# One store of ScalarE in place of two, and w3 in three transfers, in a decode kernel on Trainium2

## Chip, cores, metric

One core of a Trainium2 chip (trn2). The metric is the device time of one execution in microseconds (us). The program runs on one core only; runs called "fast" below are those not more than 1.5% above the fastest of the same kernel, and ratios use only them.

## What is computed

A decode step for four sequences: layer norm of x, attention over a window of cached keys and values, and a gated feed-forward block, all added to x.

```
xn  = layernorm(x)                                   # x: 4 x 1 x 640
q   = xn @ wq                                        # 32 heads of 192
p   = softmax(q k^T / sqrt(192))                     # the last 2048 of 8192 keys, per sequence and head
a   = (p v) @ wo
f   = (silu(xn @ w1) * (xn @ w3)) @ w2               # 640 -> 1536 -> 640
out = x + a + f                                      # 4 x 1 x 640, bf16
```

The K and V windows are 2 x 32 loads of 3.1 MB; with the weights the kernel reads 223 MB.

## The kernel before

All loads but the small one of x, which ScalarE issues, are issued by SyncE (`nc.sync.dma_start`) from a hand-written schedule. w1, w3 and w2 take turns in one buffer (a pool with one slot). w1 and w3 are loaded in two pieces each: rows of 2 and of 3 times 1536 bf16 values per partition, that is 6144 and 9216 bytes.

```python
    def ffn_load(name, w):
        wt = fpool.tile([P, KC, F], BF16, tag="w", name=name)      # KC = 5, F = 1536
        for k0, k1 in ((0, KC // 2), (KC // 2, KC)):
            nc.sync.dma_start(out=wt[:, k0:k1, :].rearrange("p k n -> p (k n)"),
                              in_=w.rearrange("(p kc) n -> p kc n", kc=KC)[:, k0:k1, :].rearrange("p k n -> p (k n)"))
        ffn[name] = wt
    # ... (cut)
    add(15, 0, ffn_load, "w3", B_w3)      # issued in slot 15 of the schedule
    add(23, 7, ffn_in, "w3")              # used in slot 23
```

The result is accumulated in PSUM in two halves of 320 columns: the first in partitions 0 to 3, the second in partitions 32 to 35. At the end two engines cast the halves and two queues store them:

```python
    NR = CT + B                                                     # CT = 32, B = 4, N0 = 320
    res = [ppool.tile([NR, N0], BF16, tag="pr", name="res") for _ in range(2)]
    nc.scalar.copy(out=res[1][CT:NR, :], in_=acc[CT:NR, :])         # ScalarE (ACT)
    nc.vector.tensor_copy(out=res[0][0:B, :], in_=acc[0:B, :])      # VectorE (DVE)
    out_v = out.rearrange("b s d -> (b s) d")
    nc.scalar.dma_start(out=out_v[:, N0:D], in_=res[1][CT:NR, :])
    nc.sync.dma_start(out=out_v[:, 0:N0], in_=res[0][0:B, :])
```

One thing is not in the source. The library gives each transfer one of eight completion semaphores in turn ("lanes" below, numbers 100, 102, 103, 106, 107, 108, 109, 110 in the trace). A transfer waits until the one eight places earlier on the same lane has landed. At the end of the program SyncE waits for the lanes in a fixed order, two semaphores at a time, and (109, ..) and (110, ..) are the last two waits. Before the change there are 88 transfers; the two stores are the last and fall on lanes 109 and 110.

Of the kernel before, what the change touches and what calls it, by code (L numbers as in the profile page):

```python
# [11 lines left out]
BF16 = mybir.dt.bfloat16  # L12
# [38 lines left out]
def kernel(  # L51
# [19 lines left out]
    nc = tc.nc  # L71
    P = 128
    B, Sq, D = A_x.shape
    _, H, Sk, Dh = A_k_cache.shape
    W = min(4096, max(256, Sk // 4))
    F = B_w1.shape[1]
    KC = D // P
# [9 lines left out]
    CT = 32  # L87
# [3 lines left out]
    N0 = D // 2  # L91
# [16 lines left out]
    ppool = ctx.enter_context(tc.tile_pool(name="pr", bufs=PBUFS))  # L108
# [36 lines left out]
    for k0 in range(0, KC, 2):  # L145
        n = min(2, KC - k0)
        wt = vpool.tile([P, 2, H * Dh], BF16, tag="vt")
        nc.sync.dma_start(out=wt[:, 0:n, :].rearrange("p k n -> p (k n)"),
                          in_=wq_v[:, k0:k0 + n, :].rearrange("p k n -> p (k n)"))
# [77 lines left out]
    acc = ps_acc.tile([P, N0], FP32, name="acc")  # L227
# [120 lines left out]
    hT = const.tile([P, FC, CT], BF16, name="hT")  # L348
    ffn = {}

    def ffn_load(name, w):
        wt = fpool.tile([P, KC, F], BF16, tag="w", name=name)
        for k0, k1 in ((0, KC // 2), (KC // 2, KC)):
            nc.sync.dma_start(out=wt[:, k0:k1, :].rearrange("p k n -> p (k n)"),
                              in_=w.rearrange("(p kc) n -> p kc n", kc=KC)[:, k0:k1, :].rearrange("p k n -> p (k n)"))
        ffn[name] = wt
# [33 lines left out]
    def add(slot, phase, fn, *args):  # L390
        sched[slot].append((phase, len(sched[slot]), fn, args))
# [28 lines left out]
    for hg in range(NG - 2):  # L420
        a = ((hg + 1) * HG - 1) * GQ + L + 3
        add(hg * HG * GQ + 8, 0, wo_load, hg)
        add(a, 6, ge_proj, hg, 0, RPP // 2)
        add(a + 1, 6, ge_proj, hg, RPP // 2, RPP)
    add(3, 0, ffn_load, "w1", B_w1)
    add(11, 7, ffn_in, "w1")
    add(11, 9, ffn_silu)
    add(15, 0, ffn_load, "w3", B_w3)
    add(23, 7, ffn_in, "w3")
    add(23, 9, ffn_h)  # L430
    add(16, 6, x_add, 0)
# [19 lines left out]
        for phase, _, fn, args in sorted(sched[s], key=lambda e: (e[0], e[1])):  # L451
            fn(*args)

    NR = CT + B
    res = [ppool.tile([NR, N0], BF16, tag="pr", name="res") for _ in range(2)]
    nc.scalar.copy(out=res[1][CT:NR, :], in_=acc[CT:NR, :])
    nc.vector.tensor_copy(out=res[0][0:B, :], in_=acc[0:B, :])
    out_v = out.rearrange("b s d -> (b s) d")
    nc.scalar.dma_start(out=out_v[:, N0:D], in_=res[1][CT:NR, :])
    nc.sync.dma_start(out=out_v[:, 0:N0], in_=res[0][0:B, :])  # L460


# [28 lines left out]
```

## Time and profile before

| | before |
|---|---|
| time, median of 3 runs | 526.6 us (526.47 to 526.67) |
| span of the profiled run | 524.4 us |
| busy share of the DMA engines' time, load queue | 99.2% |
| PE (TensorE), DVE (VectorE), ACT (ScalarE) busy | 69%, 66%, 9% of the span |

The page of the kernel before shows what limits it: the DMA row and the GB/s row (the span in 40 equal slices, 9 means 90% or more busy), the load queue q1 with its share of the time of 16 engines, and the chain of waits that ended last.

```profile
DMA  9999999999999999999999999999999999999996
GB/s 385 426 441 429 426 431 436 427 435 429 433 427 437 431 428 437 427 431 436 429 430 439 423 439 429 433 429 435 429 429 435 432 429 435 429 435 431 424 428 258
DMA packets 12285, 223.26 MB, mean 426 GB/s; under 512 B 1373, under 2 KB 1513, under 8 KB 3177
...
q1 hardware_dynamic: 12248, 222.96, 99.2%
...
DMA 61%; DVE 21%; PE 15%; ACT 2%; issue 1%; SPq 0%
DMA kt<-in_A_k_cache_dram 52%; DVE pr L244 14%; PE ps L255 8%; DMA vt<-in_A_v_cache_dram 4%; DMA w<-in_B_w_dram 4%; DVE sc L263 3%; PE qps L210 3%; PE po L328 3%; DMA x_sb<-in_A_x_dram 1%; DVE z L299 1%; ACT ex L291 1%; PE mt L285 1%; ACT L
```

The DMA engines are busy in all slices but the last, and the chain is mostly DMA. The compute engines wait: the waits of the kernel before (engine, line, what it waited for: total us, times, longest) have DVE idle for 108.5 us before its products until K has landed.

```profile
DVE pr L244 <- DMA kt<-in_A_k_cache_dram: 108.5, 29, 8.3
```

So a change can gain here in three ways: less work for the DMA engines, fewer gaps in their supply, or a shorter tail after the last load. The tail of the kernel before, from the timeline (start, duration, engine, line, operation; `ACTq` and `SPq` are the issue of a transfer by that engine's queue):

```profile
520.99 0.71 PE L231 MATMUL acc<-w,hT 128*4 128x320 bf16 x8 [0.15 <-DMA w<-in_B_w_dram]
...
521.73 0.48 DVE L457 CAST res<-acc 4x320 bf16<-4x320 f32 x1 [2.07 <-PE acc L231]
521.76 0.42 ACT L456 CAST res<-acc 4x320 bf16<-4x320 f32 x1 [4.59 <-PE acc L231]
522.21 0.28 ACTq L459 DMA_DIRECT2D out_dram<-res  x1
522.24 0.35 SPq L460 DMA_DIRECT2D out_dram<-res  x1
```

Stretches of the last loads of the kernel before, one us each (after the time: busy us of PE, PEld, DVE, ACT, POOL; then granted clock, DMA share, GB/s):

```profile
518.00:519.00 1.00, 1.00 (x21) 0.66 (x17) 0.17 (x1) 0.00 (x0) 0.00 (x0) 1.00 0.65 268
519.00:520.00 1.00, 0.45 (x10) 0.18 (x6) 0.62 (x2) 0.00 (x0) 0.00 (x0) 1.00 0.50 205
520.00:521.00 1.00, 0.84 (x14) 0.44 (x12) 0.00 (x0) 0.00 (x0) 0.00 (x0) 1.00 0.40 154
521.00:522.00 1.00, 0.70 (x8) 0.33 (x7) 0.27 (x1) 0.24 (x1) 0.00 (x0) 1.00 0.00 1
```

The DMA engines do not end together: in the last three us of loads the share falls from 0.65 to 0.40, because some engines have finished their part of the last transfers before others: the 16 counts of the last w2 load came between 518.01 and 521.35 us. The remainder of the tail is not on the page. The records of DMA packets and semaphores in the same trace give it:

```
store by ACT (lane 109): 4 packets of 640 B start 522.975 ... 523.051; last count 523.414
store by SP  (lane 110): 4 packets of 640 B start 523.074 ... 523.148; last count 523.593
SyncE passes its wait for 109 at 523.43, for 110 at 523.61; barriers until 524.43
```

The issue of the w3 loads (two, at 65.84 us) on SyncE's queue is followed by a long pause of that queue:

```profile
65.20 0.55 SPq L132 DMA_DIRECT2D vt<-in_A_v_cache_dram  x1
65.84 1.02 SPq L354 DMA_DIRECT2D w<-in_B_w_dram  x2
83.02 0.54 SPq L125 DMA_DIRECT2D kt<-in_A_k_cache_dram  x1
```

(L125, L132 and L354 are the lines of `load_k`, `load_v` and `ffn_load`.)

### The profile page before, as it was taken

To read this page: it belongs to the slowest core of one execution; us is meant where nothing else is said; L and a number is where in the kernel's file an instruction comes from. 1 tells how busy PE (TensorE), PEld (TensorE's weight loads), DVE (VectorE), ACT (ScalarE), POOL (GpSimd) and SP (SyncE) were. 2 spreads that over 40 slices of the span, in tenths; PEclk is the share of its full clock that TensorE was granted. 3 is DMA by queue.
4 is the path that set the end of the run, shared out by engine and by line. 5 is a ranking of instruction groups with operands and counts; after the bars stand their busy time and mean duration, and the time that the engine had idled before them with its cause. 6 is when DMAs were issued, how large, how long until landed. Compare 5 with 4: busy or idle time off the path is not lost.

```text
span 524.4 us, 4738 instructions
## 1 busy us (share of the span) xinstructions
PE 359.4 (69%) x2306; PEld 73.8 (14%) x1613; DVE 346.0 (66%) x435; ACT 46.0 (9%) x144; POOL 1.1 (0%) x8
## 2 busy tenths in 40 slices
PE   0965966577746767667658767676686876685785
PEld 0000211111111111111111111111111111111122
DVE  3179755479657767677656876577666866677681
ACT  2111201000000000000000000000000000000001
POOL 0000000000000000000000000000000000000000
PEclk9979878969878999789887988699878898889888
DMA  9999999999999999999999999999999999999996
GB/s 385 426 441 429 426 431 436 427 435 429 433 427 437 431 428 437 427 431 436 429 430 439 423 439 429 433 429 435 429 429 435 432 429 435 429 435 431 424 428 258
DMA packets 12285, 223.26 MB, mean 426 GB/s; under 512 B 1373, under 2 KB 1513, under 8 KB 3177
## 3 DMA queue, kind: packets, MB, share of 16 engines
q1 hardware_dynamic: 12248, 222.96, 99.2%
q8 instruction: 15, 0.25, 0.2%
q14 instruction: 6, 0.04, 0.0%
q10 hardware_dynamic: 16, 0.01, 0.0%
HBM read 222.96 MB, written 0.01 MB: 425 GB/s over the span
## 4 chain that ended last, share of the span: by engine, by line
DMA 61%; DVE 21%; PE 15%; ACT 2%; issue 1%; SPq 0%
DMA kt<-in_A_k_cache_dram 52%; DVE pr L244 14%; PE ps L255 8%; DMA vt<-in_A_v_cache_dram 4%; DMA w<-in_B_w_dram 4%; DVE sc L263 3%; PE qps L210 3%; PE po L328 3%; DMA x_sb<-in_A_x_dram 1%; DVE z L299 1%; ACT ex L291 1%; PE mt L285 1%; ACT L291 0%; DVE oT L336 0%; DVE og L333 0%
## 5 line engine op out<-in xcount | busy, mean ns | idle before, releaser
L255 PE MATMUL ps<-pr,idb 128*128 128x512 bf16 x768 | 219.4, 429 | 146.2 <-DVE pr L244 146.1
L244 DVE TENSOR_TENSOR pr<-kt,qbc 128x3072 bf16<-128x3072 bf16 x128 | 223.4, 1746 | 108.5 <-DMA kt<-in_A_k_cache_dram 108.5
L263 DVE TENSOR_REDUCE sc<-ps 128x16 f32<-128x512 f32 x128 | 87.1, 680 | 2.3 <-PE ps L255 2.3
L307 PE MATMUL o_ps<-vt,z 128*8 128x384 bf16 x1024 | 54.4, 350 | 0.2 <-DVE z L299 0.2
L328 PE MATMUL po<-o_sb,sel_w 128*32 128x192 f32 x128 | 49.2, 518 | 0.6 <-ACT o_sb L310 0.6
L307 PEld LDWEIGHTS <-z 128*8 128x8 bf16 x1024 | 24.9, 90 | 91.4 <-issue 80.0
L310 ACT COPY o_sb<-o_ps 128x384 f32<-128x384 f32 x32 | 15.3, 479 | 187.2 <-PE o_ps L307 187.2
L299 DVE TENSOR_TENSOR z<-ex,mask_b 128x256 bf16<-128x256 bf16 x32 | 13.5, 423 | 25.6 <-ACT ex L291 25.6
L288 ACT COPY negm<-mt 128x1 f32<-128x1 f32 x32 | 5.1, 159 | 259.5 <-PE mt L285 259.5
L272 PEld LDWEIGHTS mt<-idf,lmax 128*1 128x1 f32 x32 | 3.5, 108 | 142.8 <-issue 141.8
L328 PEld LDWEIGHTS po<-o_sb,sel_w 128*32 128x32 f32 x128 | 14.0, 132 | 30.8 <-issue 29.3
L255 PEld LDWEIGHTS <-idb 128*128 128x128 bf16 x124 | 11.9, 96 | 38.1 <-issue 31.6
L210 PE MATMUL qps<-wt,xnT 128*128 128x512 bf16 x59 | 16.0, 433 | 0.6 <-DVE xnT L201 0.6
L285 PEld LDWEIGHTS mt<-ones_ff,gneg 1*128 1x128 f32 x64 | 9.4, 182 | 46.1 <-issue 21.6
L277 DVE TENSOR_REDUCE gmax<-mt 1x4 f32<-1x128 f32 x32 | 8.8, 276 | 7.2 <-PE mt L272 7.1
L216 DVE CAST qbc<-qps 128x512 bf16<-128x512 f32 x6 | 3.8, 684 | 13.4 <-PE qps L210 13.4
L285 PE MATMUL mt<-ones_ff,gneg 1*128 1x1 f32 x64 | 12.1, 256 | 0.6 <-DVE gneg L280 0.6
L315 PEld LDWEIGHTS po<-rsum,tot_w 128*32 128x32 f32 x64 | 4.4, 108 | 53.6 <-ACT ex L291 27.8
L272 PE MATMUL mt<-idf,lmax 128*1 128x128 f32 x32 | 11.5, 359 | 0.0
L291 ACT ACTIVATE ex<-sc,negm 128x64 bf16<-128x64 f32 x32 | 11.1, 348 | 1.0
L231 PE MATMUL acc<-wo_t,oT 128*4 128x320 bf16 x96 | 9.3, 298 | 0.5 <-DMA wo_t<-in_A_wo_dram 0.5
L199 PE MATMUL xnT_ps<-idb,xn 4*128 4x4 bf16 x5 | 0.4, 178 | 12.0 <-DVE xn L194 12.0
(53 smaller groups left out, 69.2 us busy)
## 6 DMA issues: line engine op xcount, KB each, us to landing
kt<-in_A_k_cache_dram SPq DMA_DIRECT2D x32, 3072.0 KB, 19.9
vt<-in_A_v_cache_dram SPq DMA_DIRECT2D x30, 3072.0 KB, 27.1
wo_t<-in_A_wo_dram SPq DMA_DIRECT2D x8, 960.0 KB, 21.0
wt<-in_A_wq_dram SPq DMA_DIRECT2D x2, 3072.0 KB, 13.1
vt<-in_A_v_cache_dram SPq DMA_DIRECT2D x4, 1536.0 KB, 23.2
w<-in_B_w_dram SPq DMA_DIRECT2D x2, 1152.0 KB, 32.5
wt<-in_A_wq_dram SPq DMA_DIRECT2D x1, 1536.0 KB, 19.6
w<-in_B_w_dram SPq DMA_DIRECT2D x2, 768.0 KB
```

What stands on the lines that cost most here:

```text
L210: nc.tensor.matmul(qp[:], lhsT=xnT[:, kc].rearrange("p a b -> p (a b)"), rhs=wq_rows[kc][:, (c0 + i) * QC:(c0 + i + 1) * QC], start=(kc == ...
L231: nc.tensor.matmul(acc[i * CT:i * CT + B, :], lhsT=lhsT, rhs=rhs[:, i * N0:(i + 1) * N0], start=first, stop=last)
L244: nc.vector.tensor_tensor(out=pr[:], in0=kts[h][:, g * JQ:(g + 1) * JQ, :], in1=qbc[:, h * Dh:(h + 1) * Dh].unsqueeze(1).to_broadcast([P, ...
L255: nc.tensor.matmul(ps[:], lhsT=idb[:], rhs=pr[:, :, kk * DD:(kk + 1) * DD], start=(kk == 0), stop=(kk == NK - 1))
L263: nc.vector.tensor_reduce(out=scs[h][:, g * JQ:(g + 1) * JQ], in_=pss.pop(u)[:], axis=AX.X, op=ALU.add)
L272: nc.tensor.transpose(out=mt[0:1, 0:P], in_=chs[h][0][:], identity=idf[:])
L285: nc.tensor.matmul(mt[:, P:P + 1], lhsT=gneg[:].rearrange("o p b -> o (p b)"), rhs=ones_ff[:], start=True, stop=True)
L291: nc.scalar.activation(out=ex[:], in_=scs.pop(h)[:], func=ACTF.Exp, bias=negm[:, 0:1], scale=SCALE, accum_out=rsum[:])
L299: nc.vector.tensor_tensor(out=z[:], in0=ex[:].unsqueeze(2).to_broadcast([P, NJ, B]), in1=mask_b[:].unsqueeze(1).to_broadcast([P, NJ, B]), ...
L307: nc.tensor.matmul(o_ps[c * CT:c * CT + 2 * B, :], lhsT=z[:, 2 * jj:2 * jj + 2, :], rhs=vt[:, 2 * jj:2 * jj + 2, :], start=(jj < 4), stop= ...
L310: nc.scalar.copy(out=o_sb[:], in_=o_ps[:])
L328: nc.tensor.matmul(po[sl, 0:Dh], lhsT=sel_w[:, par].rearrange("p a b -> p (a b)"), rhs=o_sb[:, par * Dh:(par + 1) * Dh].rearrange("p (r i) ...
```

## The change

Its intent: one transfer of whole rows in place of two half-row transfers from two queues, with one completion at the end instead of two; and one more load for w3, which among other things keeps the number of transfers at 88.

```diff
-    def ffn_load(name, w):
+    def ffn_load(name, w, *at):
         wt = fpool.tile([P, KC, F], BF16, tag="w", name=name)
-        for k0, k1 in ((0, KC // 2), (KC // 2, KC)):
+        for k0, k1 in zip((0,) + at, at + (KC,)):
 ...
-    add(3, 0, ffn_load, "w1", B_w1)
+    add(3, 0, ffn_load, "w1", B_w1, KC // 2)
-    add(15, 0, ffn_load, "w3", B_w3)
+    add(15, 0, ffn_load, "w3", B_w3, KC // 2, KC - 1)
 ...
-    NR = CT + B
-    res = [ppool.tile([NR, N0], BF16, tag="pr", name="res") for _ in range(2)]
-    nc.scalar.copy(out=res[1][CT:NR, :], in_=acc[CT:NR, :])
-    nc.vector.tensor_copy(out=res[0][0:B, :], in_=acc[0:B, :])
-    out_v = out.rearrange("b s d -> (b s) d")
-    nc.scalar.dma_start(out=out_v[:, N0:D], in_=res[1][CT:NR, :])
-    nc.sync.dma_start(out=out_v[:, 0:N0], in_=res[0][0:B, :])
+    res = ppool.tile([B, 2, N0], BF16, tag="pr", name="res")
+    nc.scalar.copy(out=res[:, 1, :], in_=acc[CT:CT + B, :])
+    nc.vector.tensor_copy(out=res[:, 0, :], in_=acc[0:B, :])
+    nc.scalar.dma_start(out=out.rearrange("b s d -> (b s) d"), in_=res[:].rearrange("b i n -> b (i n)"))
```

## The prediction

> **What bounds the kernel now.** The page's slice table has the DMA row at 9 (90% or more) in 39 of 40 slices, mean 426 GB/s; the queue table gives the load queue 99.2% of the 16 engines' time. The chain of waits is 61% DMA, mostly kt loads. PE (69%) and DVE (66%) have slack. The trace's packet records fit a line: 6144 B take 234 ns, 9216 B 347 ns, 12288 B 460 ns, so about 8 ns per packet plus bytes at 27 B/ns. Only three things can move the time: the DMA engines' work, a gap in their supply, or the tail after the last load.
>
> The tail, from the timeline: last w2 piece landed at 521.35 us, last matmul ends 521.70, the two casts (ACT 0.42, DVE 0.48 us) end 522.18 and 522.21, both stores are issued at 522.21 (ACT queue) and 522.24 (SP queue), their packets run 522.98 to 523.18, SyncE's end-of-program waits see the ACT store at 523.43 and the SP store at 523.61, and barriers run until 524.43.
>
> **w3 in three transfers.** Same bytes and order. The 128 packets of 9216 B become 128 of 6144 and 128 of 3072 B (estimate from the fit: 234 + 121 = 355 ns instead of 347). With 8 rows per engine that is 8 x 8 ns plus one more completion write of 9 ns, about 0.07 us of DMA time per engine. DMA is full, so this can reach the end: +0.07 us. The extra issue costs SyncE's queue about 0.5 us near 67 us, where it then idles until 83 us: free. w3 lands by 99 us and is first used at about 117 us, so PE gains nothing from finer pieces. Completion semaphores rotate over eight lanes; one more load shifts them, but near w3 the transfer eight back has long landed, and at the end the distance of eight is unchanged (one store fewer, one load more: still 88 transfers, and the store stays on the last lane waited for). The waits of the last wo and w2 loads (490.2, 497.5, 501.1, 504.8 us) stay.
>
> **One store.** The SP issue (0.35 us, parallel) goes. The casts write disjoint columns of four partitions. I expect no ordering between them: the q casts of ACT and DVE into one tile overlap in the timeline (21.28 to 21.87 and 21.50 to 22.19). The ScalarE store must now also wait for DVE's cast: issue at 522.25 to 522.30 instead of 522.21. The Trainium skill, "DMA: Bandwidth & Descriptors", section "Issuing engines are not separate DMA queues", says different issuers share the same 16 DMA engines, so two queues save only issue time; the trace agrees: SP's 640 B packets follow ACT's. Now four packets of 1280 B (55 ns, as the x load shows) replace eight of 640 B (29 ns). Completion should be seen at 523.47 to 523.55 instead of 523.61: -0.05 to -0.15 us.
>
> **Sum.** +0.07 - 0.10, about -0.03 us: inside the spread of the runs (0.2 us). Predicted 526.5 us, 8 in 10 between 526.2 and 526.9. Faster by over 2%: 0.003; within 2%: 0.994; slower by over 2%: 0.003.
>
> **Right if:** the same DMA share and GB/s; 3072 B packets at about 121 ns; last w2 landing within 0.3 us of 521.35; casts overlapping; store issued 0.03 to 0.1 us after DVE's cast; final completion 0.05 to 0.15 us earlier relative to the last matmul.
>
> **Wrong if:** the two casts are serialized by their common tile (+0.45 us); the shifted lanes make a load wait and the DMA row drops below 9 between 67 and 120 us; a single store takes over 1.4 us from issue to completion; or the uneven finish of the DMA engines (DMA share 0.65, 0.50, 0.40 in the last three us of loads) changes.

## The result, and the profile after

After: 526.51 us median of 6 runs (526.30 to 526.79). Before, with the three runs beside it: 526.48 us median of 6 (526.26 to 526.67). Ratio 1.000, 95% interval 0.9988 to 1.0013. A ratio here and below is the mean time of one kernel's fast runs over that of the other's of the same rounds, so it is not quite the ratio of the medians quoted.

The page after, the same rows:

```profile
DMA  9999999999999999999999999999999999999996
GB/s 388 422 441 427 431 429 434 427 435 429 435 427 432 434 428 437 427 433 431 433 428 441 423 437 429 433 431 433 426 434 431 434 433 431 431 431 432 425 427 260
DMA packets 12420, 223.26 MB, mean 426 GB/s; under 512 B 1384, under 2 KB 1520, under 8 KB 3440
...
q1 hardware_dynamic: 12384, 222.96, 99.2%
...
DMA 64%; DVE 21%; PE 12%; ACT 1%; issue 1%; SPq 0%
DMA kt<-in_A_k_cache_dram 52%; DVE pr L244 15%; PE ps L255 7%; DMA vt<-in_A_v_cache_dram 4%; DMA wt<-in_A_wq_dram 4%; DMA w<-in_B_w_dram 4%; DVE sc L263 3%; PE po L328 3%; PE qps L210 1%; DVE z L299 1%; ACT ex L291 1%; DVE oT L336 1%; PE mt
```

Busy share and GB/s are those of before; q1 has 136 packets more (128 of data, 16 completions for the extra load, less 8 of SyncE's store). The split of the chain between PE and DMA differs by three points, with equal spans; the chain alone is no measure of time here.

The tail after, from the timeline. `SPq` has gone from it:

```profile
520.99 0.71 PE L231 MATMUL acc<-w,hT 128*4 128x320 bf16 x8 [0.19 <-DMA w<-in_B_w_dram]
...
521.73 0.48 DVE L456 CAST res<-acc 4x320 bf16<-4x320 f32 x1 [4.51 <-PE acc L231]
521.77 0.42 ACT L455 CAST res<-acc 4x320 bf16<-4x320 f32 x1 [7.01 <-PE acc L231]
522.29 0.27 ACTq L457 DMA_DIRECT2D out_dram<-res  x1
```

The stretches of the last loads, as before:

```profile
518.00:519.00 1.00, 0.49 (x8) 0.18 (x4) 0.00 (x0) 0.00 (x0) 0.00 (x0) 1.00 0.65 270
519.00:520.00 1.00, 0.18 (x4) 0.13 (x5) 0.00 (x0) 0.00 (x0) 0.00 (x0) 1.00 0.48 196
520.00:521.00 1.00, 0.81 (x14) 0.41 (x11) 0.00 (x0) 0.00 (x0) 0.00 (x0) 1.00 0.41 159
521.00:522.00 1.00, 0.70 (x8) 0.33 (x7) 0.27 (x1) 0.23 (x1) 0.00 (x0) 1.00 0.00 0
```

And from the packet and semaphore records of this trace:

```
last w2 load counted complete: before 521.353, after 521.351
store by ACT (lane 110): 4 packets of 1280 B start 523.052, .094, .146, .197; last count 523.585
SyncE passes its wait for 110 at 523.60; barriers until 524.41
w3: 128 packets of 3072 B took 121 ns each, 256 of 6144 B 234 ns (w1 still has 128 of 9216 B, 347 ns)
```

From the end of the last matmul to SyncE's last wait for a store is 1.912 us before and 1.901 us after. The last load lands at the same time. In the tail nothing has moved by more than a tenth of a microsecond. Earlier, SyncE's queue issues three w3 loads in its pause, and single issues there shift by up to a microsecond (the v load from 65.20 to 66.26 us); this does not make the last load land later:

```profile
66.26 0.55 SPq L132 DMA_DIRECT2D vt<-in_A_v_cache_dram  x1
66.90 1.49 SPq L354 DMA_DIRECT2D w<-in_B_w_dram  x3
82.78 0.54 SPq L125 DMA_DIRECT2D kt<-in_A_k_cache_dram  x1
```

### The profile page after: what moved, and what is told of

Same layout as the page of the kernel before. It is cut to its first block, busy times and chain, and to the rows that moved or that the text cites. A ratio compares the mean times of both kernels' runs of the same rounds, so it can differ in the third digit from the quotient of the medians.

```text
span 524.4 us, 4737 instructions
## 1 busy us (share of the span) xinstructions
PE 357.6 (68%) x2306; PEld 73.9 (14%) x1613; DVE 345.4 (66%) x435; ACT 46.0 (9%) x144; POOL 1.1 (0%) x8
## 3 DMA queue, kind: packets, MB, share of 16 engines
q1 hardware_dynamic: 12384, 222.96, 99.2%
## 4 chain that ended last, share of the span: by engine, by line
DMA 64%; DVE 21%; PE 12%; ACT 1%; issue 1%; SPq 0%
DMA kt<-in_A_k_cache_dram 52%; DVE pr L244 15%; PE ps L255 7%; DMA vt<-in_A_v_cache_dram 4%; DMA wt<-in_A_wq_dram 4%; DMA w<-in_B_w_dram 4%; DVE sc L263 3%; PE po L328 3%; PE qps L210 1%; DVE z L299 1%; ACT ex L291 1%; DVE oT L336 1%; PE mt L285 0%; ACT L291 0%; DVE og L333 0%
## 5 line engine op out<-in xcount | busy, mean ns | idle before, releaser
L255 PE MATMUL ps<-pr,idb 128*128 128x512 bf16 x768 | 216.0, 423 | 144.7 <-DVE pr L244 144.7
L307 PE MATMUL o_ps<-vt,z 128*8 128x384 bf16 x1024 | 56.8, 362 | 0.2 <-DVE z L299 0.2
L210 PE MATMUL qps<-wt,xnT 128*128 128x512 bf16 x59 | 14.9, 410 | 1.3 <-DMA wt<-in_A_wq_dram 0.6
```

What stands on the lines that cost most here:

```text
L210: nc.tensor.matmul(qp[:], lhsT=xnT[:, kc].rearrange("p a b -> p (a b)"), rhs=wq_rows[kc][:, (c0 + i) * QC:(c0 + i + 1) * QC], start=(kc == ...
L255: nc.tensor.matmul(ps[:], lhsT=idb[:], rhs=pr[:, :, kk * DD:(kk + 1) * DD], start=(kk == 0), stop=(kk == NK - 1))
L307: nc.tensor.matmul(o_ps[c * CT:c * CT + 2 * B, :], lhsT=z[:, 2 * jj:2 * jj + 2, :], rhs=vt[:, 2 * jj:2 * jj + 2, :], start=(jj < 4), stop= ...
```

## The experiments

The question is whether the two sides are really as small as the sum says, or two larger effects cancel. In the table, "tail" is the stretch from the end of the last matmul to SyncE's passing of its last wait for the stores; "load" is when the last w2 load was counted complete. Each is read from one profile.

| kernel | stores, transfers | tail us | load us | ratio to before (95%) |
|---|---|---|---|---|
| before | 2, 88 | 1.912 | 521.35 | |
| after | 1, 88 | 1.901 | 521.35 | 1.0000 (0.9988 to 1.0013) |
| after_again | 1, 88 | 1.896 | 521.46 | 1.0000 (0.9985 to 1.0015) |
| after_five | 1, 88 | 1.894 | 521.31 | 0.9998 (0.9986 to 1.0011) |
| store_only | 1, 87 | 1.965 | 521.25 | 1.0002 (0.9986 to 1.0019) |
| w3_only | 2, 89 | 2.012 | 521.42 | 1.0004 (0.9989 to 1.0019) |
| stores_both_act | 2, 88 | 2.081 | 521.30 | one run, 526.67 us |
| store_by_sp | 1, 88 | 1.896 | 521.28 | one run, 526.30 us |
| nine_casts | 1, 88 | 5.410 | 521.61 | 1.0067 (1.0050 to 1.0083) |

### after_again: the changed kernel once more

No edit.

> The changed kernel unaltered, to see how well one profile's tail repeats. Theory A (two terms far below the spread, both at the very end or on full DMA engines): time ratio to before 0.999 to 1.001; the stretch from the end of the last matmul to SyncE's sight of the last store 1.90 us within 0.03; last w2 load landed at 521.2 to 521.6 us; store issued 0.08 us after DVE's cast ends. Rival B (the kernel before and after differ by two real effects of some tenths that happen to cancel): the landing of the last load stays later than before's by 0.1 us or more, and the tail stays shorter by as much.

526.44 us median of 4 runs, before 526.33 of 7. The tail repeats to 0.005 us; the landing of the last load moves by 0.1 us from run to run. Store issued 0.082 us after DVE's cast ended. Rival B asks for the tail to stay shorter by as much as the load is later, a tenth or more: the tail is shorter by 0.016 us only. What holds is theory A.

### after_five: the same with five rounds

> The changed kernel once more beside it, with five rounds. Theory A: ratio to before 0.9993 to 1.0007; tail 1.90 us within 0.02. Rival B (two real effects of some tenths): ratio off 1 by more than 0.001, or a tail shorter than before's by 0.1 us.

526.35 us median of 5 runs, before 526.46 of 9; ratio 0.9998. The tail is 1.894 us. The measured ratio lies in A's range, though the interval is wider than that range; rival B's shorter tail by 0.1 us is excluded by three profiles.

### store_only: the store alone

```diff
-    add(15, 0, ffn_load, "w3", B_w3, KC // 2, KC - 1)
+    add(15, 0, ffn_load, "w3", B_w3, KC // 2)
```
(against the changed kernel)

> Only the single store; w3 in two transfers as before, so 87 transfers and the store's completion falls on the lane one before the last that the end of the program waits for. Theory A: ratio 0.999 to 1.001; tail 1.97 us (1.90 plus one more wait of 0.07 after the store is seen); last w2 load landed where before has it, within 0.3 us. Rival B: without the w3 split the gain of the store shows alone: total 0.1 us or more below before and the tail below 1.85 us.

526.54 us median of 4 runs, ratio 1.0002. The tail is 1.965 us, 0.005 from the expectation. With 87 transfers the store is on lane 109. SyncE passes that wait at 523.835 us and then still has to go through the wait for lane 110, at 523.897. That is what the third w3 transfer is worth at the end of the program: 0.06 us. In this profile the last matmuls themselves ended 0.68 us after the last load, instead of the usual 0.34: the granted clock of TensorE was 0.50 and 0.57 of full speed in two us of the end. It hit this one profiled execution and is not an effect of the edit, as far as one profile can tell:

```profile
518.00:519.00 1.00, 1.00 (x13) 0.52 (x9) 0.17 (x1) 0.00 (x0) 0.00 (x0) 0.50 0.62 255
519.00:520.00 1.00, 1.00 (x11) 0.49 (x8) 0.63 (x2) 0.00 (x0) 0.00 (x0) 0.57 0.53 214
520.00:521.00 1.00, 1.00 (x20) 0.65 (x16) 0.00 (x0) 0.00 (x0) 0.00 (x0) 1.00 0.34 128
```

### w3_only: the third transfer alone

```diff
-    res = ppool.tile([B, 2, N0], BF16, tag="pr", name="res")
-    ... (the one store)
+    NR = CT + B
+    ... (the two casts and two stores of before)
```
(against the changed kernel)

> Only w3 in three transfers; two stores as before, so 89 transfers, and the SyncE store's completion falls on a lane that the end of the program waits for in the middle of its list. Theory A: ratio 0.999 to 1.001; 128 packets of 3072 B at 121 ns; tail 2.03 us (SyncE store seen at about the same time as before, then two more waits of 0.07 each). Rival B: the w3 split alone makes the last load land 0.1 us or more later than in before.

526.56 us median of 4 runs, ratio 1.0004. The 3072 B packets took 121 ns each. The tail is 2.012 us: SyncE's store is now on lane 100, SyncE waits for it until 523.68 and then passes 109 and 110 at 523.71 and 523.78. So the lane a last transfer falls on is worth as much as all else in this change. Rival B (load later by 0.1 us) is not refuted by this run alone: its load landed at 521.42, 0.07 us after before's. Over all profiles the kernels with w3 in two pieces had 521.25 to 521.35 and those with three 521.28 to 521.61; the ranges overlap, and 0.07 us cannot be told from it. What small packets cost is measured with larger doses below (fine_packets to aligned_packets); the 0.07 us of w3 itself was never seen in a time.

### stores_both_act: two stores, one queue

```diff
-    nc.sync.dma_start(out=out_v[:, 0:N0], in_=res[0][0:B, :])
+    nc.scalar.dma_start(out=out_v[:, 0:N0], in_=res[0][0:B, :])
```
(against the kernel before)

> The kernel before with both stores issued by ScalarE's queue. Theory A (two queues save only the issue time of the second store): the second store is issued about 0.3 us after the first, and the tail from the last matmul to SyncE's sight of the last store grows from 1.91 to 2.1 to 2.25 us. Rival D (one queue or two, the packets decide): tail 1.88 to 1.95 us.

One run, 526.67 us. The timeline of this kernel has the second store issued 0.37 us after the first:

```profile
521.67 0.48 DVE L457 CAST res<-acc 4x320 bf16<-4x320 f32 x1 [3.08 <-PE acc L231]
521.71 0.42 ACT L456 CAST res<-acc 4x320 bf16<-4x320 f32 x1 [5.59 <-PE acc L231]
522.15 0.27 ACTq L459 DMA_DIRECT2D out_dram<-res  x1
522.52 0.26 ACTq L460 DMA_DIRECT2D out_dram<-res  x1
```

The tail is 2.081 us, a little under A's range and well outside D's. So the second queue of the kernel before was worth 0.17 us (one profile): it already let the second store run beside the first, so that taking that store away could gain little.

### store_by_sp: the one store by SyncE

```diff
-    nc.scalar.dma_start(out=out.rearrange("b s d -> (b s) d"), in_=res[:].rearrange("b i n -> b (i n)"))
+    nc.sync.dma_start(out=out.rearrange("b s d -> (b s) d"), in_=res[:].rearrange("b i n -> b (i n)"))
```
(against the changed kernel)

> The changed kernel with its one store issued by SyncE instead of ScalarE. Theory A: SyncE's issue takes 0.35 us instead of 0.27 and its completion was seen later after the last packet in before (0.42 against 0.34 us), so the tail is 1.95 to 2.10 us instead of 1.90. Rival D (the packets decide): 1.88 to 1.93 us.

One run, 526.30 us. The tail is 1.896 us: theory A's detail was wrong and rival D right. SyncE's issue does take 0.35 us, but the first packet starts 0.774 us after the issue starts, against 0.758 us for ScalarE, and the last count comes 0.333 us after the end of the last packet, like ScalarE's 0.335. The 0.416 us of SyncE's store in before was therefore not a trait of that queue. It is 0.414 us in w3_only, where the two stores again come from two queues and follow each other at once, and 0.338 us in stores_both_act, where they are 0.37 us apart. So it goes with two stores in flight together; by which mechanism is open.

### nine_casts: a longer tail

```diff
-    nc.scalar.copy(out=res[:, 1, :], in_=acc[CT:CT + B, :])
+    for _ in range(9):
+        nc.scalar.copy(out=res[:, 1, :], in_=acc[CT:CT + B, :])
```
(against the changed kernel)

> The changed kernel with ScalarE's cast of the result made nine times over (same output), a large dose of tail. Theory A (the tail is on the critical path one to one): eight more casts of 0.3 to 0.42 us each put the store 2.5 to 3.6 us later and the time up by as much, ratio to before 1.0045 to 1.007. Rival E (the end of the program waits for something else, so the tail's length is hidden): ratio below 1.002.

530.03 us median of 4 runs, before 526.41 of 7: 3.62 us more, ratio 1.0067. The timeline shows the tail:

```profile
521.98 0.48 DVE L457 CAST res<-acc 4x320 bf16<-4x320 f32 x1 [2.83 <-PE acc L231]
522.01 4.00 ACT L456 CAST res<-acc 4x320 bf16<-4x320 f32 x9 [5.36 <-PE acc L231]
526.05 0.28 ACTq L458 DMA_DIRECT2D out_dram<-res  x1
```

The tail grew from 1.90 to 5.41 us, by 3.51, and the time by 3.6. The tail is on the critical path one to one at this size; that 0.01 us off the tail is also 0.01 us off the time is concluded from it and too small to be seen.

### fine_packets: a large dose of small packets

```diff
-        wo_t = wopool.tile([P, RPP * D], BF16, tag="wo")
+        wo_t = wopool.tile([P, RPP * 2, N0 + 16], BF16, tag="wo")        # 12 packets of 640 B a row
-        wt = fpool.tile([P, KC, F], BF16, tag="w", name=name)
+        wt = fpool.tile([P, KC * HG, FW + 16], BF16, tag="w", name=name) # 20 packets of 768 B a row
         ... (loads and uses follow)
```
(against the changed kernel)

> A large dose of what the w3 split adds: padded tiles for wo, w1 and w3, so that the same bytes move in packets of 640 B (wo, 12 for one of 7680 B) and 768 B (w1 and w3, 20 a row). Theory A (DMA engines are full, every ns of packet time reaches the end): 29 ns x 12 = 348 instead of 291 ns, x 8 rows x 8 loads = 3.65 us, and about 36 x 20 = 725 instead of 581 and 589 ns, x 8 rows = 2.2 us: total +5.9 us, ratio to before 1.009 to 1.013. Rival C (the DMA engines have slack that hides small additions, which is why +0.07 us did not show): ratio below 1.004.

537.49 us median of 4 runs, before 526.33: 11.2 us more, ratio 1.0212 (1.0196 to 1.0227). Rival C falls: small additions are not hidden. But A's size was off by almost two. The packets of 640 and 768 B took 34.9 and 39.3 ns on average where 29 and 36 were assumed, and the K and V packets (24576 B) rose from 914 to 919 ns, which nothing in the edit was meant to touch.

### mid_packets: the dose with sizes of known cost

```diff
-        wt = vpool.tile([P, 2, H * Dh], BF16, tag="vt")
+        wt = vpool.tile([P, 8, 3 * QC + 16], BF16, tag="vt")             # wq: 3072 B
-        wo_t = wopool.tile([P, RPP * D], BF16, tag="wo")
+        wo_t = wopool.tile([P, 2, RPP // 2 * D + 16], BF16, tag="wo")    # 3840 B
-        wt = fpool.tile([P, KC, F], BF16, tag="w", name=name)
+        wt = fpool.tile([P, KC, F + 16], BF16, tag="w", name=name)       # 3072 B
```
(against the changed kernel)

> The dose of packets again, with sizes for which the line was measured (the 640 and 768 B packets of the last dose took longer in the stream than the line says, 34.9 and 39.3 ns on average, and the time rose by 11 us where 5.9 were expected). Same bytes and transfers as the changed kernel; padded tiles cut wq, w1 and w3 into packets of 3072 B and wo into 3840 B. From the packet times measured (121 and 149 ns): wq 20 x 121 instead of 2 x 912 + 460, +136 ns a row; w1 5 x 121 instead of 581, +24; w3 605 instead of 589, +16; wo 2 x 149 instead of 291, +7 ns x 8 loads: 232 ns x 8 rows = 1.9 us. Theory A (full DMA engines, packet time reaches the end): total +1.9 us over the changed kernel, ratio to before 1.0030 to 1.0045. Rival C (small additions of packet time are hidden in slack of the DMA engines): ratio below 1.0015.

530.98 us median of 5 runs, before 526.46 of 9: 4.5 us more, ratio 1.0084 (1.0070 to 1.0098). Rival C falls again, and A's size misses again, by 2.6 us. The K and V packets again took longer, 916.8 ns on average. The padding of 32 B per piece had also moved tiles: in the kernels before and after all K, V, wq and wo tiles begin at multiples of 256 B in SBUF, here the K and V tiles begin 160 B past one (as the builds allocate them).

### moved_tiles: the addresses of mid_packets without its packets

```diff
-        wt = vpool.tile([P, 2, H * Dh], BF16, tag="vt")
+        wt_pad = vpool.tile([P, 2 * H * Dh + 128], BF16, tag="vt")
+        wt = wt_pad[:, 0:2 * H * Dh].rearrange("p (k n) -> p k n", k=2)
-        wo_t = wopool.tile([P, RPP * D], BF16, tag="wo")
+        wo_pad = wopool.tile([P, RPP * D + 32], BF16, tag="wo")
+        wo_t = wo_pad[:, 0:RPP * D]
-        wt = fpool.tile([P, KC, F], BF16, tag="w", name=name)
+        w_pad = fpool.tile([P, KC * F + 80], BF16, tag="w", name=name)
+        wt = w_pad[:, 0:KC * F].rearrange("p (k n) -> p k n", k=KC)
```
(against the changed kernel)

> Why mid_packets cost 4.5 us where 1.9 were expected. Its padding also moved the K, V, wq and wo tiles in SBUF: in the changed kernel all of them begin at multiples of 256 B, there at 160 B past one (fine_packets: 128 B past one). This run has the tiles at exactly the addresses of mid_packets, with unused bytes at the tiles' ends and every load in the whole packets of the changed kernel. Theory F (the destination's place in SBUF costs DMA time): the 24576 B packets average 916 ns or more (914.3 in the changed kernel), ratio to before 1.003 to 1.007. Rival G (the number of packets costs more in the stream than the line says): 914.0 to 914.8 ns, ratio 0.999 to 1.001.

528.93 us median of 5 runs, before 526.28 of 9: 2.65 us more, ratio 1.0048 (1.0034 to 1.0062). Same packets as the changed kernel, same bytes, same transfers; only the places in SBUF differ. The K and V packets took 917.5 ns on average. Theory F holds, G falls. The trace has a control of its own: w1, w2 and w3 lie where they lay, and their packets took what they took in the changed kernel (6144 B 234.1 ns, 9216 B 347.0, 5120 B 196.1), while those into the moved tiles took 3 to 4 ns longer whatever their size (24576 B 917.5 instead of 914.1 ns, 12288 B 463.1 instead of 460.0, 7680 B 295.8 instead of 292.0). So over these three sizes the cost is one per packet and not per byte. And 1.9 us of packets plus 2.65 us of place is 4.55 us, against 4.52 measured in mid_packets. That the sum meets it so closely is partly luck: the 3072 B packets there took 126.6 ns on average and not the 121 assumed, and a part of the packet time is counted twice (see aligned_packets). The page of this kernel: as many packets as after, but fewer GB/s:

```profile
GB/s 387 427 437 422 437 425 429 431 433 423 431 434 424 434 422 438 424 435 424 430 432 430 427 431 430 427 433 425 430 427 435 429 432 424 434 427 430 423 423 253
DMA packets 12420, 223.26 MB, mean 424 GB/s; under 512 B 1384, under 2 KB 1520, under 8 KB 3440
...
q1 hardware_dynamic: 12384, 222.96, 99.1%
```

The Trainium skill, "DMA: Bandwidth & Descriptors", section "How a descriptor splits into AXI transactions", states that a descriptor not starting at a multiple of 256 B spends extra beats at its start; it states it for reads. In this run the sources in HBM were where they had been, and the destinations moved. The trace agrees with the direction, 24576 B packets longer by 0.37%; no run here shows the beats.

### aligned_packets: the dose with every start at a multiple of 256 B

```diff
-        wo_t = wopool.tile([P, RPP * D], BF16, tag="wo")
+        wo_t = wopool.tile([P, RPP, D + 128], BF16, tag="wo")            # 6 packets of 1280 B
-        wt = fpool.tile([P, KC, F], BF16, tag="w", name=name)
+        wt = fpool.tile([P, KC, F + 128], BF16, tag="w", name=name)      # 5 packets of 3072 B
```
(against the changed kernel)

> The dose of packets with every tile and every packet starting at a multiple of 256 B in SBUF: wo in packets of 1280 B (6 for one of 7680 B), w1 and w3 in packets of 3072 B. From the measured packet times (55 and 121 ns): wo 330 instead of 291 ns, 39 x 64 = 2.5 us; w1 +24 x 8 = 0.19, w3 +16 x 8 = 0.13 us: +2.8 us. Theory A with F: ratio to before 1.004 to 1.0067, all 3072 B packets at 121 ns. Rival G: about 2.4 times the sum as in mid_packets, +6.7 us, ratio 1.010 to 1.015. Rival C (slack hides packet time): below 1.002.

528.17 us median of 5 runs, before 526.28: 1.9 us more, ratio 1.0034 (1.0022 to 1.0047): its middle lies under A's range of 1.004 to 1.0067, the interval overlaps it, and lies above C's and under G's. The recorded packet times are those of the line: all 1280 of 3072 B took 121 ns, the wo packets 55. The sum of all packet times shows where the remaining third went. It is worked out from the packet records within the span of the profile: "packet time" is all durations added and divided by 16; "overlap" is what was under way beyond 16 packets at once, and "idle" what was missing to 16, both summed over time and divided by 16. Packet time less overlap plus idle is the span.

| kernel | packet time per engine | overlap | idle | span |
|---|---|---|---|---|
| before | 521.1 us | 2.8 us | 6.1 us | 524.4 us |
| after | 521.0 | 2.8 | 6.2 | 524.4 |
| moved_tiles | 523.3 | 2.7 | 6.3 | 526.9 |
| mid_packets | 526.0 | 3.5 | 6.5 | 529.1 |
| aligned_packets | 523.9 | 3.9 | 6.0 | 526.0 |
| fine_packets | 535.6 | 6.7 | 6.7 | 535.7 |

Here 2.9 us of packet time were added to the changed kernel's (2.8 expected) and 1.6 us came out in the span. Of the 1.3 us between them, 1.1 us is overlap and only 0.2 us is less idle time. There was no slack to fill: in the kernel before, from 2.2 to 517.8 us, there is no moment with fewer than 16 packets under way, and the idle time lies at the two ends. The overlap is a matter of the records: for nearly every packet another one starts 3 or 4 ns before its record ends (the trace does not name the engine, so that this is the next packet on the same one is concluded from the numbers). Each added packet therefore counts 3 to 4 ns twice. So added packet time reaches the end, but a further packet costs about 4 to 5 ns of it, not the 8 ns of the prediction's line (an estimate: 8 less 3 to 4). The page of this kernel shows the higher share, which contains the overlap:

```profile
DMA packets 18180, 223.26 MB, mean 424 GB/s; under 512 B 1384, under 2 KB 7664, under 8 KB 9328
...
q1 hardware_dynamic: 18144, 222.96, 99.4%
```

The experiments point to no version that is measurably better than both kernels: every part of this change that was taken away or exchanged is worth under 0.2 us of 526.

## Why the prediction was right

- What binds. The load queue has 99.2% of the DMA engines' time before and after, and the page's rows are the same. Shown, and confirmed from the other side by the dose runs: added packet time lengthens the kernel.
- w3 in three transfers, +0.07 us. The recorded time per packet was as worked out (121 ns for 3072 B, 234 + 121 instead of 347 ns: 128 rows x 8 ns / 16 engines = 0.064 us). That it reached the end could not be seen; the last load landed at 521.351 instead of 521.353 us, and it landed anywhere from 521.31 to 521.46 in three profiles of the changed kernel. From aligned_packets about 0.04 us of it is to be expected at the end, because nearly half of the 8 ns is counted twice; that is an estimate (0.07 x 1.6 / 2.9). So this term was probably too large as well.
- Lanes. The waits of the last loads stayed: the last two w2 loads were issued at 501.12 and 504.77 us in both. The store stayed on the last lane. store_only and w3_only show that this point, a side remark of the prediction, is worth 0.06 to 0.1 us by itself.
- The casts into one tile. They overlap as predicted (DVE 521.73 to 522.21, ACT 521.77 to 522.18), and the store was issued at 522.294, in the predicted 522.25 to 522.30.
- One store, -0.05 to -0.15 us: this term of the sum was mis-sized. Completion was "seen at 523.47 to 523.55" in the prediction; it was seen at 523.60, so the gain was 0.01 us (0.011, 0.016 and 0.018 in three profiles). The condition "final completion 0.05 to 0.15 us earlier" thus failed. The issue came 0.084 us later than ScalarE's before, as foreseen. What was mis-sized is the time of the packets. ScalarE's store of before was seen 1.22 us after its issue, and 1.22 us added to the predicted issue gives 523.47 to 523.52 us; the prediction does not show its working, but its range fits this. The four packets of 1280 B, however, ran 0.198 us from the first start to the last end, where ScalarE's four of 640 B ran 0.105 us. They start about 48 ns apart, the eight of both old stores 25 ns apart, so that four and eight take the same 0.20 us. What the one store did gain was the completion: 0.335 us after the last packet instead of 0.416. So +0.084 - 0.004 - 0.081 = -0.001 us at the last count, to which the measured -0.008 comes with the 0.007 us by which the first packet followed the issue sooner.

The Trainium skill's sentence on issuing engines, cited in the prediction, agrees with the runs: two queues issued the second store 0.34 us sooner after the last matmul than one queue (0.54 against 0.88 us), and half of that, 0.17 us, reached the end. Its section "Why a DMA increments its semaphore by 16 and not by 1" on the same page says that a transfer issued by SyncE or ScalarE that runs on k engines gets the other 16 - k counts at once from the sequencer and one from each engine as its data lands. The trace agrees for the store of four partitions: its semaphore is written once at 522.739 us, before any packet, and then four times from 523.439 to 523.585.

The net of the two parts is then within a few hundredths of zero, in a kernel whose runs spread by 0.6 us. The prediction of no change was right for the reason it gave, with the store's gain put about 0.1 us too high. The time alone did not test this: an error of that size in either term would have left the number right, and only the traces show it.

## What to carry to other kernels

Before merging two small stores into one, look whether they already run beside each other: here they did, and merging them gained 0.01 us, since the merged store had to wait for the slower of two casts and its larger packets took as long as all the small ones. The count and order of transfers can matter more than their content at the end of a program, since the last waits go through the semaphores in a fixed order. Where the DMA engines are full, look at the addresses of the destinations too: moving tiles from multiples of 256 B to 160 B past one (one of the two wo tiles to 224 B) cost 2.65 us, more than anything this change did. Other distances were not tried by themselves.

## What the Trainium skill lacked or had wrong

- "DMA: Bandwidth & Descriptors", "How a descriptor splits into AXI transactions": it names the start of reads only. Moving the destinations in SBUF from multiples of 256 B to 160 B past one made the kernel 0.48% slower (526.28 to 528.93 us) and the 24576 B packets 917.5 instead of 914.1 ns.
- Same page, "Anatomy of one DMA — SWDGE (gpsimd) path": the fixed 2.0 us is fitted for GpSimd's path. The page has no such whole time for a transfer from ScalarE's or SyncE's queue. For a 5 KB store from ScalarE's it was 1.29 us from the start of the issue (522.294) to the last count (523.585), and the last count came 0.335 us after the last packet ended.
- No page has it: of two stores in flight together from two queues the second's last count came 0.414 to 0.416 us after its last packet; alone, or 0.37 us behind the other, 0.333 to 0.338 us.
- No page has these recorded durations by packet size: the packets of this kernel followed 8 ns plus 27 B per ns from 1280 to 24576 B (55, 121, 149, 234, 347, 460, 912 ns for 1280, 3072, 3840, 6144, 9216, 12288, 24576 B), but packets of 640 and 768 B in the stream (fine_packets, whose pieces lie 672 and 800 B apart, so that most begin at no multiple of 256 B) took 34.9 and 39.3 ns on average, where that line gives 32 and 36. The records overlap by 3 to 4 ns with the next packet, 2.8 us per engine in the kernel before and 3.9 us in aligned_packets, so that their sum overstates the engines' time.
